# One hand-ordered block for phase 1, paced z2 sums, Sqrt for the first rows, z1 weights loaded during the row DFT, merged loads of the weight tails

## The chip, the cores and the metric

One core of a Trainium2 chip runs the whole program. The metric is device microseconds of one execution, the median over fast runs. Ratios are the mean time of one kernel's fast runs over the mean time of the kernel before's fast runs in the same rounds, so they are not quite the ratio of the medians quoted beside them. A ratio counts as faster or slower beyond 2%; a difference smaller than that can still be clear of noise, and the interval tells.

## The reference

Cut to what matters: a layer norm over the rows of x (2048 rows of 576), then two branches.

```python
xn = _layernorm(x, axis=-1)
# branch A: rfft2 over (rows, columns), times W, irfft2
s = irfft2(rfft2(xn) * (w_r + 1j * w_i))
# branch B: gated MLP
z  = gelu(xn @ w_in)                 # 576 -> 4608
z1 = z[..., :2304];  z2 = _layernorm(z[..., 2304:])
g  = w_sp @ z2 + b_sp                # 2048 x 2048 over the rows
b  = (z1 * g) @ w_out
return x + s * silu(b)
```

All inputs and the output are bfloat16.

## The kernel before

It works in phases. Phase 0 normalises x, transposes it and does the row DFT (`p0`), one group per block of 128 rows, 16 groups. The column DFT and its inverse follow (`p1` to `p5`, through buffers in HBM), then the large product with `w_sp`. Between these, `fill(n)` puts n chunks of the z2 or z1 product on TensorE, to keep it busy. The change is aimed at everything up to the column DFT. In the code and the views, PE is TensorE, DVE VectorE, ACT ScalarE, POOL GpSimd and SP SyncE, whose queue issues most loads here; `DMA` is the work of the core's 16 DMA engines, which move the bytes.

The feature dimension 576 is cut into four blocks of 128 and a tail of 64. The tail has 32 rows of each half of `w_in`, and it is held twice, so that two chunks can share the array. Loading one block of weights takes two large loads and four of 32 rows:

```python
wv = [B_w_in[a * H2:a * H2 + 2 * P, :].rearrange("(b p) f -> p b f", p=P) for a in range(2)]
def load_win(t, fs):
    for a in range(2):
        nc.sync.dma_start(out=t[:, a:KS - 1:2, :], in_=wv[a][:, :, fs])
        for r in range(2):
            nc.sync.dma_start(out=t[r * KT + a * HT:r * KT + (a + 1) * HT, KS - 1, :],
                              in_=B_w_in[a * H2 + 2 * P:(a + 1) * H2, fs])

XC = [load_x(0)]
for g in range(3):                       # z2 weights and x in turn, all from SP's queue
    load_win(WIN2[...g...], ...)
    XC.append(load_x(g + 1))
nc.sync.dma_start(out=G1, ...)
```

The rstd (one over the standard deviation) of each row block is made on POOL, by an add and a pow:

```python
def rstd_of(mv, n, tag):
    ...
    nc.gpsimd.tensor_scalar(out=ve[:], in0=mv[:, :, 1], scalar1=1e-5, ...)
    nc.gpsimd.tensor_tensor(out=rs[:], in0=ve[:], in1=mhalf[:, 0:n], op=ALU.pow)
```

Phase 0 and phase 1 are two blocks of manual order. The z1 weights are loaded at the start of the second one, behind the reads of the row buffer:

```python
with tc.manual_schedule(engines={SP, PE, DVE}):
    ...                                  # warm-up, first rows
    for m in range(2, MT):
        xpose(m + 1); p0_fold(m); ln1([m + 3]); ln1_apply(m + 2)     # cut: bounds
        fill(2 if m == 3 else 1, norm=False)
        p0(m)
with tc.manual_schedule(engines={SP, PE, DVE}):
    for ch in range(4):
        p1_read(ch)
    load_win1(0); load_w(0); load_win1(1)
    fill(12)
    for s2 in range(0, N2, 2):
        p1(s2)
        fill(1)
```

## Time and profile before

| | before |
|---|---|
| time, median of 6 runs | 518.15 us (516.71 to 519.33) |
| PE busy, of a span of 516.2 us | 501.6 us (97%) |
| first transpose, third and last p0 group start at | 7.07, 14.91, 43.00 us |
| first p1 group starts at | 53.16 us |

The first view lists what TensorE waited for: who, for whom, us in total, how many times, the longest.

```profile
PE pt L283 <- DVE AR L272: 4.2, 9, 1.4
PE ph L483 <- DMA AR<-in_B_w_in_dram: 3.2, 1, 3.2
```

The transposes (`pt`) wait for VectorE's apply, and the first z1 chunk (`ph L483`) waits 3.2 us for its weights. The second view is a table of stretches of time: the busy time of each engine, then the granted clock of TensorE, the mean busy share of the 16 DMA engines, and GB/s.

```profile
core 0: us, PE busy (x) PEld busy (x) DVE busy (x) ACT busy (x) POOL busy (x), PEclk, DMA share, GB/s
15.00:43.00 28.00, 25.21 (x207) 15.78 (x208) 27.08 (x95) 23.40 (x39) 20.30 (x35) 1.00 0.53 176
43.00:62.00 19.00, 15.77 (x95) 8.08 (x94) 14.12 (x27) 12.60 (x32) 6.04 (x15) 0.95 0.69 226
```

In the row DFT VectorE is busy 27.08 of 28 us, so it sets the pace there. The same table by single microseconds shows half clock after the wait for z1 weights:

```profile
60.00:61.00 1.00, 1.00 (x6) 0.53 (x4) 0.42 (x1) 0.69 (x2) 0.80 (x3) 0.57 0.77 227
61.00:62.00 1.00, 1.00 (x3) 0.30 (x2) 0.81 (x2) 0.00 (x0) 0.00 (x0) 0.50 0.69 156
62.00:63.00 1.00, 1.00 (x5) 0.60 (x4) 0.00 (x0) 0.71 (x2) 0.00 (x0) 0.50 0.34 102
```

One view also belongs here more than I saw: the timeline of SP's queue, which issues these loads. Columns are start, duration of the issue, what is loaded, and how many issues are merged in the line.

```profile
5.14 1.25 SPq L234 DMA_DIRECT2D AR<-in_B_w_in_dram  x2
6.47 0.39 SPq L224 DMA_DIRECT2D AR<-in_A_x_dram  x1
11.20 0.43 SPq L224 DMA_DIRECT2D AR<-in_A_x_dram  x1
15.55 0.79 SPq L234 DMA_DIRECT2D AR<-in_B_w_in_dram  x2
16.38 0.47 SPq L224 DMA_DIRECT2D AR<-in_A_x_dram  x1
```

An issue takes about 0.4 to 0.6 us. The three lines of `L224` are the second to fourth chunk of x; the last is issued at 16.38 us. The view of DMA issues, for that issue alone, has its size and the time to landing:

```profile
AR<-in_A_x_dram SPq DMA_DIRECT2D x1, 576.0 KB, 7.0
```

So all of x is on the chip at 23.4 us.

### The profile page before, as it was taken

How to read it: one execution, taken by the hardware profiler on the slowest of the kernel's cores; microseconds unless marked ns; L12 is line 12 of the kernel's file. 1: busy time of each engine (PE TensorE's matmuls, PEld its weight loads, DVE VectorE, ACT ScalarE, POOL GpSimd, SP SyncE). 2: the span in 40 equal slices, each digit the busy share in tenths (PEclk: the TensorE clock that was granted, in tenths of full speed). 3: DMA queues.
4: the chain of work that ended last, by engine and by line, in shares of the span. 5: the costliest groups of instructions: out<-in, count | busy, mean ns of one | idle time of the engine just before them, and what ended most of it. 6: DMA issues, size and time to landing. Idle time of an engine off the chain costs nothing.

```text
span 516.2 us, 9284 instructions
## 1 busy us (share of the span) xinstructions
PE 501.6 (97%) x3454; PEld 314.7 (61%) x3454; DVE 333.9 (65%) x715; ACT 168.0 (33%) x341; POOL 210.7 (41%) x286
## 2 busy tenths in 40 slices
PE   7989799999999999999999999999999999999996
PEld 3555355444446554356666677666566678888885
DVE  5997688545436475856656656865666637777734
ACT  3887665576567757510000001100000011000001
POOL 4683312334342586754344411334444301655500
PEclk8999899999999999999999999999999999999999
DMA  8923859977565794373121269512121655111202
GB/s 261 342 71 108 289 176 274 311 230 232 174 210 184 172 256 134 133 224 117 31 62 32 60 132 190 163 32 63 30 59 35 148 107 146 33 43 45 83 18 76
DMA packets 85949, 70.81 MB, mean 137 GB/s; under 512 B 39760, under 2 KB 78416, under 8 KB 85648
## 3 DMA queue, kind: packets, MB, share of 16 engines
q1 hardware_dynamic: 80608, 56.08, 40.3%
q0 software_dynamic: 5152, 14.11, 8.3%
q8 instruction: 27, 0.44, 0.4%
q14 instruction: 18, 0.15, 0.1%
q10 hardware_dynamic: 144, 0.03, 0.0%
HBM read 40.55 MB, written 21.26 MB: 120 GB/s over the span
## 4 chain that ended last, share of the span: by engine, by line
PE 83%; DVE 7%; DMA 5%; issue 2%; POOL 1%; ACT 1%; SPq 0%; POOLq 0%; DVEq 0%; ACTq 0%
PE pm L546 41%; PE ph L483 13%; PE ph L406 10%; PE po L600 10%; DMA AR<-in_A_x_dram 2%; DVE st L260 2%; PE pb L352 2%; PE pa L381 2%; PE pa L366 1%; DVE AR L469 1%; DMA AR<-Ad 1%; DMA AR<-in_B_w_in_dram 1%; PE pl L600 1%; PE pa L340 1%; PE pa L316 1%
## 5 line engine op out<-in xcount | busy, mean ns | idle before, releaser
L546 PE MATMUL pm<-AR,Z_74 128*128 128x384 bf16 (+1 forms) x864 | 138.7, 308 | 0.0
L550 DVE TENSOR_TENSOR AR<-pm,AR 128x384 f32<-128x384 f32 (+3 forms) x162 | 82.2, 512 | 71.9 <-PE pm L546 40.2
L546 PEld LDWEIGHTS <-Z_74 128*128 128x128 bf16 x864 | 84.5, 98 | 40.6
L546 PE MATMUL pm<-AR 128*128 128x384 bf16 (+1 forms) x648 | 107.0, 308 | 0.8 <-DVE AR L550 0.5
L406 PE MATMUL ph<-AR 128*128 128x384 bf16 (+1 forms) x480 | 90.0, 330 | 0.1
L483 PE MATMUL ph<-AR 128*128 128x512 bf16 (+1 forms) x360 | 86.0, 382 | 3.2 <-DMA AR<-in_B_w_in_dram 3.2
L546 PEld LDWEIGHTS <-AR 128*128 128x128 bf16 x648 | 63.3, 98 | 33.2 <-issue 3.0
L560 ACT ACTIVATE AR<-pm 128x384 f32<-128x384 f32 (+1 forms) x27 | 12.3, 454 | 187.7 <-PE pm L546 187.7
L534 POOL TENSOR_TENSOR AR<-Z_74,AR 128x1024 bf16<-128x1024 bf16 x27 | 57.8, 2141 | 35.0 <-PE pm L546 33.1
L600 PE MATMUL po<-AR 128*128 128x288 bf16 x540 | 66.6, 286 | 0.0
L600 PEld LDWEIGHTS <-AR 128*128 128x128 bf16 x594 | 56.9, 98 | 13.9
L406 PEld LDWEIGHTS <-AR 128*128 128x128 bf16 (+1 forms) x480 | 40.2, 98 | 37.1 <-issue 18.0
L503 POOL DMA_DIRECT2D Z1d<-AR x58 | 32.7, 563 | 69.3 <-ACT AR L492 64.9
L561 POOL TENSOR_TENSOR AR<-AR 128x384 f32<-128x384 f32 (+1 forms) x27 | 22.9, 847 | 77.0 <-ACT AR L560 77.0
L483 PEld LDWEIGHTS <-AR 128*128 128x128 bf16 (+1 forms) x360 | 30.7, 98 | 32.5 <-issue 5.2
L492 ACT ACTIVATE AR<-ph 128x512 bf16<-128x512 f32 x72 | 42.4, 595 | 17.4 <-PE ph L483 16.4
L426 ACT ACTIVATE Z_74<-ph 128x384 bf16<-128x384 f32 x72 | 33.5, 492 | 22.7 <-PE ph L406 22.4
L342 DVE TENSOR_TENSOR AR<-pa,AR 128x578 bf16<-128x578 f32 x32 | 22.8, 753 | 20.5 <-PE pa L340 20.4
L603 ACT ACTIVATE TH<-po 128x576 f32<-128x576 f32 x15 | 9.8, 651 | 78.0 <-PE po L600 78.0
L557 DVE TENSOR_TENSOR AR<-AR 128x384 bf16<-128x384 bf16 (+1 forms) x108 | 31.7, 334 | 0.9
L604 DVE SCALAR_TENSOR_TENSOR AR<-TH,po 128x576 bf16<-128x576 f32 x15 | 11.3, 752 | 30.1 <-ACT TH L603 30.1
L609 POOL DMA_DIRECT2D out_dram<-AR x12 | 6.6, 554 | 52.2 <-DVE AR L607 45.8
(101 smaller groups left out, 507.2 us busy)
## 6 DMA issues: line engine op xcount, KB each, us to landing
Z1d<-AR POOLq DMA_DIRECT2D x58, 128.0 KB, 3.2
AR<-Z1d SPq DMA_DIRECT2D x36, 192.0 KB, 3.1
AR<-in_A_x_dram SPq DMA_DIRECT2D x20, 144.0 KB, 3.1
AR<-in_B_w_out_dram SPq DMA_DIRECT2D x1, 2592.0 KB, 10.0
Ad<-AR POOLq DMA_DIRECT2D x16, 144.5 KB, 3.1
AR<-Ad SPq DMA_DIRECT2D x4, 578.0 KB, 5.8
AR<-in_A_w_r_dram SPq DMA_DIRECT2D x16, 144.5 KB, 3.9
AR<-in_A_w_i_dram SPq DMA_DIRECT2D x16, 144.5 KB, 3.9
```

Source lines behind the costliest of these rows:

```text
L342: nc.vector.tensor_tensor(out=tt[:, c, :, :], in0=pa[:, :, 0:L], in1=wt[:, c, hh % 4:hh % 4 + 2, :], op=ALU.mult)
L406: nc.tensor.matmul(self.ph[:], lhsT=xnT[rows, self.m, ks, :], rhs=WIN2[rows, ks, n * ZC:(n + 1) * ZC], start=start, stop=stop)
L426: nc.scalar.activation(out=zc, in_=ph[:], func=ACT.Gelu_apprx_tanh)
L483: nc.tensor.matmul(self.ph[:].rearrange("p (a t) -> p a t", a=4), lhsT=wb[rows, ks, (fi % WG) * P:(fi % WG + 1) * P], rhs=xnT[rows, 4 * tq ...
L492: nc.scalar.activation(out=zs, in_=ph[:], func=ACT.Gelu_apprx_tanh)
L503: (nc.sync if place[0] > len(kinds) - 16 else nc.gpsimd).dma_start(out=d, in_=s_)
L534: nc.gpsimd.tensor_tensor(out=t, in0=zblk(p, 1, 0), in1=t2, op=ALU.subtract)
L546: nc.tensor.matmul(dst, lhsT=z[:, s, :], rhs=SLB[SA[name]][:, s, 0:nt], start=(s == 0 and not more), stop=(s == HM - 1), skip_group_check= ...
L550: nc.vector.tensor_tensor(out=out, in0=x, in1=y, op=ALU.add)
L557: nc.vector.tensor_tensor(out=o, in0=o, in1=zb[:, f, h, 0:nt], op=ALU.mult)
L561: nc.gpsimd.tensor_tensor(out=p1a, in0=p1, in1=B[0], op=ALU.add)
L600: nc.tensor.matmul(pv[:, hh, :], lhsT=U[:, fi, h, i * P:(i + 1) * P], rhs=WOUT[:, fi, c0 + hh * H2:c0 + hh * H2 + w // nh], start=(fi == 0 ...
```

## The change

It means to take the z2 sums off VectorE while VectorE sets the pace, to take the wait for z1 weights away, and to start sooner. It also tidies the loads: the two 32-row loads of each copy of a weight tail become one.

```diff
+    wv = B_w_in.rearrange("(a d) f -> a d f", a=2)
     def load_win(t, fs):
         for a in range(2):
-            nc.sync.dma_start(out=t[:, a:KS - 1:2, :], in_=wv[a][:, :, fs])
-            for r in range(2):
-                nc.sync.dma_start(out=t[r * KT + a * HT:r * KT + (a + 1) * HT, KS - 1, :], in_=B_w_in[a * H2 + 2 * P:(a + 1) * H2, fs])
+            nc.sync.dma_start(out=t[:, a:KS - 1:2, :], in_=wv[a, 0:2 * P, fs].rearrange("(b p) f -> p b f", p=P))
+        for r in range(2):
+            nc.sync.dma_start(out=t[r * KT:(r + 1) * KT, KS - 1, :], in_=wv[:, 2 * P:H2, fs])
 ...
-        rs = rstd_of(mv, n, f"l1{n}")
+        if ms[0] < 2:
+            rs = small.tile([P, n], F32, tag=f"l1{n}r", bufs=5)
+            nc.scalar.activation(out=rs[:], in_=mv[:, :, 1], func=ACT.Sqrt, bias=eps[:], scale=1.0)
+            nc.vector.reciprocal(out=rs[:], in_=rs[:])
+        else:
+            rs = rstd_of(mv, n, f"l1{n}")
 ...
-    ACT_SUMS = (4, 9, 12, 14)
+    ACT_SUMS = (4, 6, 8, 12, 14)
 ...
-    def z2_stats(u):
-        while stats_q and stats_q[0][0] < u:
-            stats_q.pop(0)[1]()
+    def z2_stats(n):
+        for _ in range(n):
+            for q in (norm_q, stats_q):
+                if q and q[0][0] < tick[0]:
+                    q.pop(0)[1]()
+                    break
 ...
-            fill(2 if m == 3 else 1, norm=False)
+            fill(1, 0)
             p0(m)
-    with tc.manual_schedule(engines={SP, PE, DVE}):
+            if m in (6, 9):
+                load_win1(m // 9)
         for ch in range(4):
             p1_read(ch)
-        load_win1(0)
         load_w(0)
-        load_win1(1)
-        fill(12)
+        fill(11, 2)
```

Cut: the new order of the first rows (row 0 is applied before row 1 is summed, three chunks before the loop instead of one), the dummy Gelu that moved behind row 1, and the paces of the later fills (2 or 3 sums per chunk).

More of the change, by code (lines that the diff above doesn't have):

```diff
@@ L147 @@
     nc.scalar.dma_start(out=ident[:], in_=cd_id.ap())
-    scr = pers.tile([P, 1], F32)
-    nc.vector.memset(scr[:], 0.0)
-    nc.scalar.activation(out=scr[:], in_=scr[:], func=ACT.Gelu_apprx_tanh)
-    mhalf = pers.tile([P, MT], F32)
+    eps = pers.tile([P, 1], F32)
+    nc.vector.memset(eps[:], 1e-5)
+    mhalf = pers.tile([P, 1], F32)
     nc.gpsimd.memset(mhalf[:], -0.5)
@@ L225, in load_x @@
         return t
-    wv = [B_w_in[a * H2:a * H2 + 2 * P, :].rearrange("(b p) f -> p b f", p=P) for a in range(2)]
     HT = H2 - 2 * P
+    wv = B_w_in.rearrange("(a d) f -> a d f", a=2)
     def load_win(t, fs):
         for a in range(2):
-            nc.sync.dma_start(out=t[:, a:KS - 1:2, :], in_=wv[a][:, :, fs])
-            for r in range(2):
-                nc.sync.dma_start(out=t[r * KT + a * HT:r * KT + (a + 1) * HT, KS - 1, :], in_=B_w_in[a * H2 + 2 * P:(a + 1) * H2, fs])
+            nc.sync.dma_start(out=t[:, a:KS - 1:2, :], in_=wv[a, 0:2 * P, fs].rearrange("(b p) f -> p b f", p=P))
+        for r in range(2):
+            nc.sync.dma_start(out=t[r * KT:(r + 1) * KT, KS - 1, :], in_=wv[:, 2 * P:H2, fs])
     def load_win1(g):
@@ L413, in z2_post @@
         on_act = m in ACT_SUMS
-        if n == 0:
-            z2s[m] = small.tile([P, NZC + 3], F32, tag="sm2", name="sm2") if on_act else \
-                small.tile([P, NZC, 6], F32, tag="st2", name="st2", bufs=4)
-        st = z2s[m]
         zc = Z2[:, m, n * ZC:(n + 1) * ZC]
         if on_act:
+            if n == 0:
+                z2s[m] = small.tile([P, NZC + 3], F32, tag="sm2", name="sm2", bufs=2)
+            st = z2s[m]
             nc.scalar.activation(out=zc, in_=ph[:], func=ACT.Gelu_apprx_tanh, accum_out=st[:, n:n + 1])
@@ L426, in z2_post, with z2_sums, z2_norm @@
             nc.scalar.activation(out=zc, in_=ph[:], func=ACT.Gelu_apprx_tanh)
-            stats_q.append((tick[0], partial(nc.vector.bn_stats, out=st[:, n, :], in_=zc)))
+            stats_q.append((tick[0], partial(z2_sums, m, n, zc)))
         if n == NZC - 1:
-            stats_q.append((tick[0], partial(z2_norm, m, st, on_act)))
-    stats_q = []
-    def z2_norm(m, st, on_act):
+            stats_q.append((tick[0], partial(z2_norm, m, on_act)))
+    def z2_sums(m, n, zc):
+        if n == 0:
+            z2s[m] = small.tile([P, NZC, 6], F32, tag="st2", name="st2", bufs=4)
+        nc.vector.bn_stats(out=z2s[m][:, n, :], in_=zc)
+    stats_q, norm_q = [], []
+    def z2_norm(m, on_act):
+        st = z2s[m]
         mv = small.tile([P, 1, 2], F32, tag="mvz", bufs=3)
@@ L445, in z2_norm @@
         rs = rstd_of(mv, 1, "l2")
-        stats_q.append((tick[0] + 2, partial(nc.vector.tensor_scalar, out=Z2[:, m, :], in0=Z2[:, m, :], scalar1=mv[:, 0, 0:1],
+        norm_q.append((tick[0] + 2, partial(nc.vector.tensor_scalar, out=Z2[:, m, :], in0=Z2[:, m, :], scalar1=mv[:, 0, 0:1],
                                                    scalar2=rs[:], op0=ALU.subtract, op1=ALU.mult)))
@@ L449, in z2_norm @@
             zp = Z2[:, m, :].rearrange("p (a b f) -> p a b f", b=2, f=P)
-            stats_q.append((tick[0] + 3, partial(nc.vector.tensor_tensor, out=zp[:, :, 1, :], in0=zp[:, :, 1, :],
+            norm_q.append((tick[0] + 3, partial(nc.vector.tensor_tensor, out=zp[:, :, 1, :], in0=zp[:, :, 1, :],
                                                        in1=zp[:, :, 0, :], op=ALU.subtract)))
-    def z2_stats(u):
-        while stats_q and stats_q[0][0] < u:
-            stats_q.pop(0)[1]()
+    def z2_stats(n):
[4 more added lines that the diff above has]
+                    break
     wspv = B_w_sp.rearrange("t (b p) -> t b p", p=P)
@@ L630, in full, with fill @@
             c.mm(ks, slice(0, P), first and ks == 0, not first and ks == KS - 2)
-    def fill(n, norm=True):
+    def fill(n, pace=1):
         for _ in range(n):
@@ L653, in fill @@
                 c.post()
-            if norm:
-                z2_stats(tick[0])
+            z2_stats(pace)
     SP, PE, DVE = mybir.EngineType.SP, mybir.EngineType.PE, mybir.EngineType.DVE
@@ L668 @@
         ln1([0])
-        ln1([1])
         ln1_apply(0)
         xpose(0)
+        keep_warm(2)
+        ln1([1])
         ln1_apply(1)
+        nc.scalar.activation(out=THF[:, 0:1], in_=ln1_of[1][0], func=ACT.Gelu_apprx_tanh)
+        p0_fold(0)
         xpose(1)
-        keep_warm(2)
         ln1([2])
-        p0_fold(0)
         p0(0)
-        ln1([3])
-        ln1_apply(2)
-        xpose(2)
-        fill(1, norm=False)
-        p0_fold(1)
-        p0(1)
+        fill(1, 0)
+        ln1_apply(2)
+        p0_fold(1)
+        fill(1, 0)
+        xpose(2)
+        p0(1)
+        ln1([3])
         ln1_apply(3)
+        fill(1, 0)
         nc.sync.dma_start(out=MM, in_=cd_mm.ap().rearrange("p (a k) -> p a k", a=3))
@@ L694 @@
                 ln1_apply(m + 2)
-            fill(2 if m == 3 else 1, norm=False)
+            fill(1, 0)
             p0(m)
-    with tc.manual_schedule(engines={SP, PE, DVE}):
+            if m in (6, 9):
+                load_win1(m // 9)
         for ch in range(4):
             p1_read(ch)
-        load_win1(0)
         load_w(0)
-        load_win1(1)
-        fill(12)
+        fill(11, 2)
         for s2 in range(0, N2, 2):
@@ L712 @@
         nc.sync.dma_start(out=CESO, in_=cd_ceso.ap().rearrange("p (a c l) -> p a c l", a=NLC, c=2))
-        fill(12)
+        fill(12, 2)
         p2(0)
@@ L722 @@
             p4_read(ch)
-        fill(12)
+        fill(12, 2)
         for u in range(4 * NLC):
@@ L734 @@
         for i in range(NT // P):
-            fill(rest // 4)
+            fill(rest // 4, 2)
             slab_sums(i, 0)
-        fill(rest - 3 * (rest // 4))
+        fill(rest - 3 * (rest // 4), 3)
         nc.sync.dma_start(out=BB, in_=B_b_sp.rearrange("(a s) -> a s", a=1).to_broadcast((P, S)))
-        fill(len(kinds) - place[0])
+        fill(len(kinds) - place[0], 3)
         z1_store(None, None)
-        z2_stats(10 ** 6)
+        assert not stats_q and not norm_q
         for w in (0, 2, 1):
```

## The prediction

> **What bounds the kernel now.** TensorE: the page has PE busy 501.6 of 516.2 us, and the chain of waits is 83% PE. After 64 us PE hardly stops, and nothing moves on it there. What can be won lies before, in three places.
>
> 1. *Row DFT, 15 to 43 us.* The table by stretches has DVE busy 27.1 of 28 us. The chain runs through `st L260` (DVE); `pt L283` waits for `L272` nine times, 4.2 us. The timeline gives one p0 group per 2.16 us (14.91 to 43.00, 13 steps); where PE is not held, 1.69. From start to start DVE spends per row 0.73 on statistics, 0.11 on the aggregate, 0.5 on the apply, 0.4 on the fold, and 0.46 on a z2 `BATCH_NORM_STATS2` that the scheduler hoisted here from the second block (12 in the loop).
> 2. *z1 weights.* PE waits 3.23 us for `in_B_w_in`, up to 58.8 us; these loads were issued at 50 us behind four 578 KB reads. Then the granted clock is 0.5 from 59.9 to 63.3 us, which costs half of that, 1.7 us. The Trainium skill ("TensorE: Matmul & The Clock Gate", What's actually happening) says that idle TensorE drops to half clock, in windows of about 3.4 us; this trace agrees.
> 3. *Start.* The first x row lands at 3.1 us, the first transpose starts at 7.07; POOL's pow holds `L272` for 1.48 us. But the second x chunk lands only at 12.56, and DVE waits for it.
>
> **What changes, costed.**
> - No z2 sums in phase 0: DVE loses 12 x 0.46 = 5.5 us, falling to 1.75 us a row. But PE needs 1.69 + 0.56/4 = 1.83, ACT about 1.8, POOL 1.5 to 1.9 (its pow takes 0.56 us alone, 0.88 beside busy DVE). I expect 1.90 to 1.95 us a step: 13 x 0.24, about 3.2 us. The sums move to 43 to 76 us, where DVE has slack; at most 0.5 us comes back.
> - z1 weights issued at p0 6 and 9, when DMA is 20% busy: the 3.2 us wait and 1.7 us of half clock both go.
> - Sqrt on ACT plus reciprocal replaces POOL's 1.9 us for row 0: first transpose near 5.2 us. A second table load (1.28 us) precedes the first Gelu, largely hidden. As z2 weights and x land at 10 to 12 us (DMA is at its limit from 4 us), about 1 us survives to the third p0.
> - 11 chunks instead of 12 before the first column step: the Ad read landed 8.7 us after phase 0; 11 chunks cover about 8.6. Loss at most 0.3.
> - One more row of sums on ACT: 4 us where ACT is 66% busy; free.
>
> **Sum.** 3.2 + 4.9 + 1.0 + 0.3 (last rows) less 0.5 = about 9 us, nearly all on the critical path: 509.2 us, range 505.8 to 513.0. Faster by over 2%: 0.32; within 2%: 0.67; slower: 0.01.
>
> **What would show it.** First transpose at 5 to 5.5 us; third p0 about 1 us earlier; p0 step 1.9 to 1.95 us; `pt <- L272` under 2 us; last p0 at 38.5 to 39.8 us; no PE wait for `in_B_w_in`, no half clock around 60 us; PE after 76 us as long as before, shifted by 8 to 10 us.
>
> **What would make it wrong.** PE reaches its floor of 1.83 us a row (over 11 us in all). ACT or POOL limits at 2 us or more. PE waits for z2 weights near 9 us, with a longer half-clock window. Moved sums hold DVE's evacuations in p1, or 11 chunks do not cover Ad's read.

## More of the kernel before

Last, the page counts packets:

```profile
DMA packets 85949, 70.81 MB, mean 137 GB/s; under 512 B 39760, under 2 KB 78416, under 8 KB 85648
```

## The result, and the profile after

The changed kernel took 517.44 us (10 runs, 514.83 to 519.51) against 518.03 us of the kernel before (20 runs, 515.48 to 519.97). The ratio is 0.9993, with an interval of 0.9973 to 1.0014: the same. About 9 us had been expected.

The waits of TensorE after:

```profile
PE pt L287 <- DVE AR L276: 4.7, 5, 2.6
PE ph L410 <- DMA AR<-in_B_w_in_dram: 4.1, 3, 1.9
```

The wait for z1 weights (`L483` before) has gone, but a wait of 4.1 us for the z2 weights (`L410`) has come, and the waits for VectorE's apply have grown to 2.6 us. VectorE in turn waits for x, four times:

```profile
DVE st L259 <- DMA AR<-in_A_x_dram: 8.6, 4, 3.0
```

Before, this wait was 2.5 us, of which 2.0 us were for the very first row. The table of stretches says where the time lies:

```profile
15.00:43.00 28.00, 24.33 (x188) 14.78 (x188) 21.72 (x79) 21.18 (x35) 17.63 (x33) 0.94 0.74 214
43.00:62.00 19.00, 19.00 (x133) 10.96 (x133) 16.15 (x38) 15.21 (x37) 5.51 (x11) 1.00 0.57 195
```

From 43 us on TensorE is full, as intended. Up to 43 us it does less than before (188 matmuls instead of 207), although VectorE is no longer full (21.72 us). In short: the first p1 group starts at 57.27 instead of 53.16 us, 4.1 us later; from there to the end it is 457.5 instead of 463.0 us, 5.5 us shorter. The change gained in one place and lost in another.

The chain of waits, in order of time (start, length, what), shows what stood in the way:

```profile
9.75 3.08 SPq L233
12.88 1.96 SPq L223
14.89 1.97 SPq L231
...
22.04 14.01 DMA AR<-in_A_x_dram
36.07 0.83 DVE st L259 x2
```

The chain runs through SP's own issues. The timeline of SP's queue, to be held against the one of before:

```profile
4.06 1.30 SPq L233 DMA_DIRECT2D AR<-in_B_w_in_dram  x2
5.40 0.47 SPq L223 DMA_DIRECT2D AR<-in_A_x_dram  x1
6.03 2.67 SPq L231 DMA_DIRECT2D AR<-in_B_w_in_dram  x2
8.74 4.10 SPq L233 DMA_DIRECT2D AR<-in_B_w_in_dram  x2
12.88 1.96 SPq L223 DMA_DIRECT2D AR<-in_A_x_dram  x1
17.61 4.38 SPq L233 DMA_DIRECT2D AR<-in_B_w_in_dram  x2
22.04 2.33 SPq L223 DMA_DIRECT2D AR<-in_A_x_dram  x1
```

There are fewer issues than before, but from 6 us on most take some 1 to 3 us each instead of 0.4. The first merged pair, at 4.06 us, took only 1.30 us for two issues, near the 1.25 of a split pair before. So a merged load is not slow to issue in itself; the issues behind it are. The last chunk of x is issued at 22.04 instead of 16.38 us, and lands 14.0 us later, at 36.05 us, instead of 7.0 us later, at 23.4.

One might think that all the DMA engines were full. From 8 to 13 us they were (a share of 1.04 to 1.14; this view goes a little above 1). But at 13 to 15 us, while the core still waited, they were not. The table by microseconds, after:

```profile
13.00:14.00 1.00, 0.00 (x0) 0.00 (x0) 0.48 (x2) 0.18 (x1) 0.00 (x0) 1.00 0.48 152
14.00:15.00 1.00, 0.42 (x4) 0.10 (x3) 0.00 (x0) 0.06 (x1) 0.00 (x0) 1.00 0.15 52
```

and before:

```profile
13.00:14.00 1.00, 1.00 (x11) 0.58 (x9) 0.97 (x6) 0.77 (x2) 0.27 (x1) 1.00 1.09 294
14.00:15.00 1.00, 0.89 (x6) 0.21 (x6) 0.97 (x4) 1.00 (x4) 0.92 (x3) 1.00 1.07 300
```

Between 14 and 15 us the core waits for data, and the mean busy share of its 16 DMA engines is 0.15 where it was 1.07. Two busy engines of 16 would give 0.125. What TensorE waited for then was the tails themselves: 3.5 of its 4.1 us of waits end at matmuls of 64 rows, which read them.

```profile
12.33 0.32 PE L410 MATMUL ph<-AR 64*128 64x384 bf16 x1 [1.59 <-DMA AR<-in_B_w_in_dram]
14.58 0.48 PE L410 MATMUL ph<-AR 64*128 64x384 bf16 x3 [1.93 <-DMA AR<-in_B_w_in_dram]
```

The packet count points the same way:

```profile
DMA packets 85409, 70.81 MB, mean 138 GB/s; under 512 B 39220, under 2 KB 77876, under 8 KB 85108
```

The bytes are the same, but there are 540 small packets fewer, for 18 loads fewer (36 tail loads became 18). If each load ends with one small packet per DMA engine that it uses, 36 x 16 = 576 became 18 x 2 = 36: exactly 540 fewer. On this reading a merged load uses 2 engines.

The Trainium skill has the rule in "DMA: Bandwidth & Descriptors", in the section on why a DMA increments its semaphore by 16 and not by 1: the number of engines k is set by each access pattern's slowest dimension that is not 1, as the largest k up to 16 that divides the slowest dimension of both. The merged source is 2 x 32 x columns: its slowest dimension is 2. I had not looked this up for a load that moves so little. Another page, "Perfetto Trace Analysis" (DMA Instruction — HWDGE), says that the reported duration lasts until all descriptors, the single copy orders of the load, are generated and the sequencer has made its own semaphore increments, and that more descriptors may be generated than fit in the buffer. An issue that takes 2 us where it took 0.4 agrees with a queue that has no room, though no view shows the queue itself.

### The profile page after: what moved, and what is told of

It reads as the page before. It is cut to its first block, busy times and chain, and to the rows that moved or that the text cites. A ratio compares the mean times of both kernels' runs of the same rounds, so it can differ in the third digit from the quotient of the medians.

```text
span 514.8 us, 9262 instructions
## 1 busy us (share of the span) xinstructions
PE 499.8 (97%) x3454; PEld 314.3 (61%) x3454; DVE 332.5 (65%) x712; ACT 172.1 (33%) x356; POOL 209.1 (41%) x285
## 4 chain that ended last, share of the span: by engine, by line
PE 88%; DMA 4%; SPq 3%; DVE 3%; issue 1%; POOL 0%; ACT 0%; DVEq 0%; POOLq 0%
PE pm L558 42%; PE ph L495 14%; PE ph L410 13%; PE po L612 10%; DMA AR<-in_A_x_dram 3%; PE pa L385 2%; PE pb L356 2%; SPq L233 2%; DVE AR L481 1%; PE pa L370 1%; SPq L231 1%; PE pa L344 1%; PE pa L320 1%; PE pl L612 1%; DMA AR<-c_cdsd 1%; PE pa L302 1%
## 5 line engine op out<-in xcount | busy, mean ns | idle before, releaser
L410 PE MATMUL ph<-AR 128*128 128x384 bf16 (+1 forms) x480 | 90.3, 329 | 4.1 <-DMA AR<-in_B_w_in_dram 4.1
L572 ACT ACTIVATE AR<-pm 128x384 f32<-128x384 f32 (+1 forms) x27 | 12.3, 455 | 187.5 <-PE pm L558 187.5
L410 PEld LDWEIGHTS <-AR 128*128 128x128 bf16 (+1 forms) x480 | 40.4, 98 | 41.5 <-issue 22.4
L429 ACT ACTIVATE Z_74<-ph 128x384 bf16<-128x384 f32 x66 | 30.9, 491 | 24.2 <-PE ph L410 23.6
L346 DVE TENSOR_TENSOR AR<-pa,AR 128x578 bf16<-128x578 f32 x32 | 22.7, 751 | 13.6 <-PE pa L344 13.2
```

What stands on the lines that cost most here:

```text
L346: nc.vector.tensor_tensor(out=tt[:, c, :, :], in0=pa[:, :, 0:L], in1=wt[:, c, hh % 4:hh % 4 + 2, :], op=ALU.mult)
L410: nc.tensor.matmul(self.ph[:], lhsT=xnT[rows, self.m, ks, :], rhs=WIN2[rows, ks, n * ZC:(n + 1) * ZC], start=start, stop=stop)
L429: nc.scalar.activation(out=zc, in_=ph[:], func=ACT.Gelu_apprx_tanh)
```

## The experiments

Theory A: the merged tail load, being on 2 engines, keeps these busy for long; SP stands in later issues, and x and z2 weights come late. Theory B: the z1 weights, now loaded during the row DFT, take bandwidth from x. Theory C: the hand order, the pacing or Sqrt lost what the rest won.

### Tail loads split again

```diff
-        for r in range(2):
-            nc.sync.dma_start(out=t[r * KT:(r + 1) * KT, KS - 1, :], in_=wv[:, 2 * P:H2, fs])
+            for r in range(2):       # inside the loop over a
+                nc.sync.dma_start(out=t[r * KT + a * HT:r * KT + (a + 1) * HT, KS - 1, :], in_=wv[a, 2 * P:H2, fs])
```

> The changed kernel with one part undone: the 32-row tail of each weight block is loaded by two DMAs of 32 rows again, as before the change, instead of one of 2 x 32 rows. Theory A (the merged load uses only 2 of the 16 DMA engines and fills their queues, so that SP's later issues stall): SP's issues fall back to about 0.4 us, x chunk 4 to 7 lands near 12 us, the last x chunk before 25 us, PE's 4.1 us wait for z2 weights and the 2.6 us wait at 37 us go, the last p0 is at 38.5 to 40 us, and the time is 509 us (507 to 512), ratio to before 0.983. Theory B (the z1 weights loaded during the row DFT take bandwidth from x): the x chunks still land late and the time stays at 516 to 518 us. Theory C (hand order or Sqrt lost what the loads won): also 516 to 518 us.

Measured: 509.97 us against 517.19 us, ratio 0.9861 (0.9835 to 0.9887). A second time: 510.37 us, 0.985 (0.9824 to 0.9877). SP's timeline is as before the change:

```profile
6.49 0.42 SPq L223 DMA_DIRECT2D AR<-in_A_x_dram  x1
10.87 0.42 SPq L223 DMA_DIRECT2D AR<-in_A_x_dram  x1
15.72 0.43 SPq L223 DMA_DIRECT2D AR<-in_A_x_dram  x1
```

and of TensorE's waits these are left:

```profile
PE pt L287 <- DVE AR L276: 1.9, 3, 1.0
PE ph L410 <- DMA AR<-in_B_w_in_dram: 0.8, 1, 0.8
```

VectorE's wait for x is back to the 2.0 us for the first row. The last p0 group starts at 40.98 us, 1 us later than I expected. The z1 weights are still loaded early here, and order, pacing and Sqrt are as in the change, so neither theory B nor C can explain the loss. I call this kernel "all-split" below.

### Only the merged load, in the kernel before

```diff
         for a in range(2):
             nc.sync.dma_start(out=t[:, a:KS - 1:2, :], in_=wv[a][:, :, fs])
-            for r in range(2):
-                nc.sync.dma_start(out=t[r * KT + a * HT:...], in_=B_w_in[a * H2 + 2 * P:(a + 1) * H2, fs])
+        for r in range(2):
+            nc.sync.dma_start(out=t[r * KT:(r + 1) * KT, KS - 1, :], in_=wt2[:, 2 * P:H2, fs])   # wt2: "(a d) f -> a d f"
```

> The kernel before with only the merged tail load (one DMA of 2 x 32 rows in place of two of 32). Theory A: SP's issues take 2 to 5 us, x lands as late as in the changed kernel, and the time rises by 5 to 10 us to 523 to 528 us, all of it before 65 us. Theories B and C: the same time as before, 518 us, or slightly less as SP has fewer issues.

Measured: 525.6 us against 517.19, ratio 1.0164 (1.0137 to 1.0191), 8.4 us longer by the medians. The issue of the last tail pair on SP:

```profile
17.43 5.05 SPq L235 DMA_DIRECT2D AR<-in_B_w_in_dram  x2
22.53 1.68 SPq L224 DMA_DIRECT2D AR<-in_A_x_dram  x1
```

This one edit, with nothing else of the change, costs about what the change lost. The two experiments undo and do the same part, and agree within their noise: 7.4 us (the 517.44 of the changed kernel less 510.0, medians; 6.8 to 7.4 by the ratios) and 8.4 us. They do not lose it in quite the same places. In the profiles of the changed kernel, the merged loads put the first p1 group 6.6 us later (57.27 instead of 50.65) and cost nothing clear after it (0.3 us). In the kernel before they put it 5.3 us later (58.48 instead of 53.16) and cost 2.9 us after it, as the late z1 weights come by merged loads too: the wait for them is 5.4 instead of 3.2 us. I had expected all of it before 65 us.

### Merged, but with the slow dimension 32

Theory A has a rival within it: perhaps a load with one dimension more is slow to issue whatever its order. If the two halves are interleaved over the partitions, the merged load stays one load per copy with the same rows, but its source is 32 x 2 instead of 2 x 32.

```diff
-    d[2, 0:nt_] = 2 * P + np.arange(nt_)
-    d[2, nt_:2 * nt_] = H + d[2, 0:nt_]
+    d[2, 0:2 * nt_:2] = 2 * P + np.arange(nt_)
+    d[2, 1:2 * nt_:2] = H + d[2, 0:2 * nt_:2]
...
-                                in_=wv[:, 2 * P:H2, fs])
+                                in_=wv[:, 2 * P:H2, fs].rearrange("a d f -> d a f"))
...
-        out=xn[:, 4 * P:KS * P].rearrange("p (r a i) -> p r a i", r=2, a=2)
+        out=xn[:, 4 * P:KS * P].rearrange("p (r i a) -> p r a i", r=2, a=2)
```

> The changed kernel with the merged load kept as one DMA per copy, but with the two halves interleaved in the partitions, so that the slowest dimension is 32 (by 2) instead of 2 (by 32); constants and the x columns follow the new order. Theory A in its form of 16 engines against 2: as fast as with split loads, 509 us (507 to 512), with SP issues of about 0.45 us. Rival A2 (a load with one dimension more, or with more descriptors in one issue, is slow to issue whatever its order): as slow as the changed kernel, 516 to 518 us.

Measured: 510.58 us against 517.19, ratio 0.9876 (0.9853 to 0.9898). Its packets:

```profile
DMA packets 85661, 70.81 MB, mean 139 GB/s; under 512 B 39472, under 2 KB 78128, under 8 KB 85360
```

85949 less 85661 is 288 = 18 x 16: 18 loads fewer, each on 16 engines. So the same load, in the same number of issues, is fast on 16 engines and slow on 2. The number of dimensions is not the cause. That SP's issues are 0.45 us each was not quite right: at 7.34 us a tail pair took 2.08 us here, where 4.10 us were taken on 2 engines.

### Merged for z1 only

```diff
+                if fs.start >= Fh:      # z2 weights: two loads of 32 rows
+                    nc.sync.dma_start(out=t[r * KT + a * HT:r * KT + (a + 1) * HT, KS - 1, :], in_=wv[a, 2 * P:H2, fs])
+                elif a == 1:            # z1 weights: the merged load
+                    nc.sync.dma_start(out=t[r * KT:(r + 1) * KT, KS - 1, :], in_=wv[:, 2 * P:H2, fs])
```

> The changed kernel with the z2 weight tails split again and only the z1 tails merged. Theory A: the start is free of stalls as with all split; the two early z1 blocks still stall SP for some us near 25 to 35 us, but only the constants and the row-buffer reads stand behind them, so the time is within 2 us of the all-split version (509 to 511 us). Theory B: 516 to 518 us.

Measured: 509.79 us against 517.19, ratio 0.9861 (0.9831 to 0.9892), as all-split. Its issues do stall, with nothing urgent behind them:

```profile
19.63 2.34 SPq L236 DMA_DIRECT2D AR<-in_B_w_in_dram  x2
22.01 2.94 SPq L231 DMA_DIRECT2D AR<-in_B_w_in_dram  x2
```

The 12 merged loads of z1 are harmless here. What costs is the 6 at the start: x stands behind them in the same queue, and TensorE needs the tails themselves at once. The runs do not separate these two. The count of packets again fits: 85589, 360 fewer than before, which is 24 x 16 less 12 x 2.

### Where the 7.2 to 7.8 us of the all-split version come from

Three parts were undone, and one of them was done alone too. (7.2 and 7.8 are the two ratios of the all-split version.)

*z1 weights late again.* In the all-split version:

```diff
-            if m in (6, 9):
-                load_win1(m // 9)
...
             p1_read(ch)
+        load_win1(0)
         load_w(0)
+        load_win1(1)
```

> The all-split version of the changed kernel (510.0 us) with the two z1 weight blocks loaded after the row-buffer reads again, as before the change. Theory of the prediction (this part is worth the wait of 3.2 us and 1.7 us of half clock): 514 to 515.5 us, a PE wait of 3 to 5 us for the z1 weights and a window of half clock after it. Rival (the part is worth little, the gain came from the row DFT and the start): under 512 us.

Measured: 516.9 us against 517.42, ratio 0.9996 (0.9977 to 1.0015). This is 1.4 us above the range that I expected. The wait for z1 weights and the clock after it:

```profile
PE ph L495 <- DMA AR<-in_B_w_in_dram: 4.0, 1, 4.0
```

```profile
55.00:56.00 1.00, 0.00 (x0) 0.00 (x0) 0.00 (x0) 0.21 (x2) 0.00 (x0) 0.75 0.75 195
59.00:60.00 1.00, 1.00 (x5) 0.54 (x4) 0.32 (x1) 0.49 (x1) 0.00 (x0) 0.50 0.70 187
62.00:63.00 1.00, 1.00 (x7) 0.62 (x6) 0.02 (x1) 0.53 (x1) 0.60 (x1) 0.83 0.77 310
```

The first p1 group starts 2.8 us sooner than before (50.34 us), but the weights come only 2.1 us sooner (TensorE goes on at 56.70 instead of 58.78 us). The wait grows from 3.2 to 4.0 us, and half clock now lasts from about 55.5 to 62.3 us, 6.8 us instead of 3.4. In this profile 1.1 of the 2.8 us are lost again after the first p1 group. By the ratio over all runs nearly all that the row DFT had won is gone.

*z1 weights early, alone.* In the kernel before, `load_win1(m // 9)` at m = 6 and 9 instead of the two late calls.

> The kernel before with one part of the change alone: the two z1 weight blocks loaded during the row DFT (at p0 6 and 9), with split tails. Theory of the prediction: the 3.2 us wait for z1 weights and the half clock after it go, 513 us (512 to 514.5), ratio 0.990. Rival (theory B: these loads take bandwidth from x or the row-buffer writes): 516 to 518 us.

Measured: 513.85 us against 517.42, ratio 0.9942 (0.9927 to 0.9958). This alone gains 3.0 us by the ratio, not the 5 expected. The wait for z1 weights and the half clock do go, but TensorE now waits for VectorE twice in p1, and for 1.0 us at the start of the large product, where it was 0.3 us before:

```profile
PE pa L316 <- DVE AR L320: 1.2, 2, 0.6
PE pm L546 <- DVE AR L469: 1.0, 1, 1.0
```

VectorE's timeline ahead of the first wait in p1 shows a z2 sum, an aggregate and then the evacuation (`L320`) in its fixed order. Ahead of the second it shows a normalisation and a difference of 2304 and 1152 columns. The first and the last of this stretch are:

```profile
57.29 0.88 DVE L455 TENSOR_SCALAR Z<-Z,mv,rs 128x2304 bf16<-128x2304 bf16 x1 [0.34 <-POOL rs L251]
...
59.01 0.75 DVE L320 CAST AR<-pa 128x578 bf16<-128x578 f32 x1
```

The p1 waits do not occur in the all-split version, with its sums let out one or two per chunk. The wait at the large product does: it is 0.7 us in the second profile of that version. So by the ratios one part alone is worth 3.0 us, all the others without it 0.2 us, and all together 7.2 to 7.8 us. They are worth more together: without the early z1 weights the row DFT's gain falls into the wait for them, and without the pacing a part of what the weights gain falls into waits for VectorE. The second half of this is argued from the p1 waits: the pacing was not tested alone.

*Sums inside the row DFT again.* In the all-split version, one sum per chunk in the loop (14 of them; the trace of the kernel before has 15 up to the last p0 group, 12 of them up to 40 us):

```diff
-            fill(1, 0)
+            fill(1, 1)
             p0(m)
```

> The all-split version with one z2 sum let out per chunk inside the row DFT loop (14 sums there; the kernel before had 12). Theory of the prediction (DVE sets the step of the row DFT): the step between p0 groups rises from 1.99 to about 2.2 us, the last p0 is 2.5 to 3 us later and the time is 512.5 to 513.5 us. Rival (PE, ACT and POOL hold the step at 2 us anyway): 510 to 510.8 us.

Measured: 512.92 us against 517.42, ratio 0.9923 (0.9909 to 0.9937), 2.5 to 3.0 us more than all-split by the medians and 3.2 to 3.8 by the ratios. Transposes wait for VectorE again:

```profile
PE pt L287 <- DVE AR L276: 4.9, 9, 0.9
```

From the third p0 group (15.10 us) to the last (44.05 us) a step takes 2.23 us; in the all-split version it is 1.99 us (15.11 to 40.98). So VectorE did set the step, as the prediction had it.

*No Sqrt.* All-split, with POOL's pow for all rows and the first Gelu's table at the start.

```diff
-        if ms[0] < 2:
-            ... Sqrt on ScalarE, reciprocal on VectorE
-        else:
-            rs = rstd_of(mv, n, f"l1{n}")
+        rs = rstd_of(mv, n, f"l1{n}")
```

> The all-split version with the first two rows' rstd by POOL's pow again and the table of the first Gelu loaded at the start, so no Sqrt and no second table load. Theory of the prediction: first transpose near 7 us instead of 5.4, time 0.5 to 1.5 us longer (510.5 to 511.5 us). Rival (the start is set by the landing of z2 weights and x, so nothing survives): 510.0 us within 0.3.

Measured: 510.42 us against 517.42, ratio 0.9872 (0.9855 to 0.989). Repeated beside its partner:

> The all-split version without Sqrt again, now beside its partner, as the first comparison came from different calls (ratios 0.9861 and 0.9872, intervals overlapping). If Sqrt is worth what the last p0 suggested (1.05 us later in the profiles), 511.0 us; if it is worth the 0.4 us of the medians, 510.4 us.

> The all-split version again, as a partner on the same chip for the other two: 510.0 us.

511.11 us (0.9867) without and 510.37 us (0.985) with Sqrt. The intervals overlap, so 0.7 us is likely but not shown. In the profiles the third p0 group starts at 15.92 and 16.10 us without Sqrt, and at 15.11 and 14.93 with it. The first transpose starts at 6.10 us without Sqrt, not near 7.

### A version to beat both

The all-split version beats both kernels. One attempt to better it issued half of the first z2 weight group from ScalarE's queue:

```diff
-    def load_win(t, fs):
+    def load_win(t, fs, q=None):
...
+            eng = q[a] if q else nc.sync
+            eng.dma_start(out=t[:, a:KS - 1:2, :], in_=wv[a, 0:2 * P, fs].rearrange("(b p) f -> p b f", p=P))
...
+                 [nc.sync, nc.scalar] if g == 0 else None)
```

> The all-split version with half of the first z2 weight group issued from ScalarE's queue at the start instead of SP's, which leaves SP three issues fewer ahead of the second x chunk. PE waited 0.75 us near 10 us for this group, so at best 0.3 to 0.8 us less than the all-split version of the same call (509.2 to 509.7 us). Rival (the early transfers are limited by bandwidth, not by issue): the same within 0.2 us, or worse if the early weights delay the x rows.

Measured: 510.0 us, ratio 0.9848 (0.9822 to 0.9875), beside 510.37 us (0.985) of all-split. No gain is shown.

## Why the prediction was wrong

It said 509.2 us (505.8 to 513.0) and the changed kernel took 517.44. With one edit of the change taken out, it takes 510.0.

- **The step that failed** is a term that the list "What changes, costed" does not have. It goes through the sums, the z1 weights, Sqrt, the 11 chunks and the row of sums on ScalarE, and never prices the merged tail loads, the one line of the diff that looked like tidying. With it failed what stood on it: "z2 weights and x land at 10 to 12 us" took it for granted that the loads land as before. The runs showed that the merged loads cost about 7 us in the changed kernel (7.4 by the medians) and 8.4 us in the kernel before: TensorE's last wait for z2 weights ended at 14.58 us, VectorE got the second chunk of x at 16.51 us (12.56 before) and the last at 36.05 us (23.4 before). An estimate from sizes, made afterwards and with 2 engines for a merged load, would have told: ahead of and with the last x chunk stand 5043 KB on all 16 engines (576 + 435 + 2304 + 1728 KB) and 576 KB of tails. Evenly spread that is 351 KB per engine; with the tails on two engines it is 315 + 288 = 603 KB on those two, 1.72 times as much. Measured from the first issue at 0.73 us, the last x chunk came after 35.3 us instead of 22.7, 1.56 times.
- **"PE waits for z2 weights near 9 us"** was named among the risks, and it is what the profile showed (4.1 us), in three waits that ended at 9.45, 12.33 and 14.58 us, but for a reason that was not foreseen. Half clock did follow: the granted clock is 0.71 from 15 to 16 us, 0.50 for the next two and 0.59 from 18 to 19 us.
- **The row DFT** was right in mechanism: with the tails split, a step takes 1.99 us instead of 2.16, against 1.90 to 1.95 expected; with sums in the loop 2.23. The gain was over-sized by about 1 us, and the last group starts at 40.98 us instead of 38.5 to 39.8.
- **The z1 weights** were right too: no wait, no half clock in p1. The size was above the 4.9 us in the sum: with a faster row DFT the late weights cost 6.9 us (516.9 less 510.0, medians; 7.0 to 7.5 by the ratios).
- **The start** was wrong: about 1 us was to survive to the third p0 group. In two profiles of the all-split version this group starts at 15.11 and 14.93 us, against 14.91 before, although the first transpose did start at 5.45 us (5.32 in the changed kernel; 5 to 5.5 predicted). The profile of the kernel before also holds a stretch of half clock from about 8.9 to 12.3 us, which the prediction passed over. The run with early z1 weights alone has the start of the kernel before, but in its profile the clock is full there, and its third p0 group starts at 13.89 us. So at full clock the new start looks about 1 us later, not sooner; this is one profile against two. Without Sqrt the group starts at 15.92 and 16.10 us, so the new order of the first rows seems to give back what Sqrt gains, and more. The order was not tested alone.
- **"PE after 76 us as long as before"** held in the part that was checked: from the first matmul of the large product to the end it is 296.4 us before (516.2 less 219.76), 296.3 in the changed kernel and 296.1 in the all-split version. From the first p1 group to that matmul it is 161.2 us in the all-split version instead of 166.6; 4.9 of these 5.4 us are the wait for z1 weights (3.2) and half of the half clock after it (1.7).
- The sum of about 9 us was thus right within 1.2 to 1.8 us for the change without the merged loads, in part by luck. In the two profiles 2.3 to 2.5 us are won up to the first p1 group, where 4.5 were predicted (row DFT, start, last rows), and 5.2 to 5.8 us after it, where 4.4 were (z1 weights less 0.5). The two errors cancelled in part.

What stays open: the trace does not name which of the 16 DMA engines a load used. That it was two is read from the packet counts, from the busy share of 0.15, and from the 32 x 2 experiment.

## What to carry to other kernels

Merging small loads is not free of risk: look at the slowest dimension of both access patterns after the merge, and keep it a multiple of 16 (32 did here, 2 did not), since loads of 96 KB on 2 DMA engines held up every load behind them in the queue here. Read the durations of the issues themselves; where one takes 2 us instead of 0.4, as here, look for a load on few engines ahead of it, even if the mean DMA share is low. And when a gain ahead of a wait for data seems to vanish, take the wait away first: here the early z1 weights alone were worth 3.0 us and all the rest without them 0.2, but together they were worth over 7 us.

## What the Trainium skill lacked or had wrong

- "DMA: Bandwidth & Descriptors" has the rule for k and warns to use all 16 engines, but not that a load on few engines makes the *later* issues of the same queue slow: here the x chunk at 22.04 us took 2.33 us to issue instead of 0.4, and the constants `G1` behind it 2.32.
- The same page says that each engine that a load uses ends with a semaphore write of its own, but not that a trace's count of small packets tells k by it. Here it does: one per engine and load (540, 288 and 360 fewer for 18 loads on 2, 18 loads on 16, and 12 loads on 2 engines).
- "ScalarE: Activation LUTs" (What ACT_TABLE_LOAD costs) gives about 2.66 us per switch to a different table set, 1.28 us of load and about 1.38 us of drain. In the all-split version Sqrt ends at 7.12 us, the load takes 1.28 us from 7.13, and the Gelu starts at 8.43: 1.31 us in all, as in the second profile of that version. No drain is seen.
- "TensorE: Matmul & The Clock Gate" (What's actually happening) has windows of 3.4 us for half clock. A wait of 3.2 us was followed by 3.4 us of half clock, but one of 4.0 us by 6.8 us, of which 5.6 lie after TensorE's restart at 56.7 us. The page says that its windows run freely; that TensorE can so run at half clock for longer than one window after a restart is the number to add.
